# A new order table for all engines' steps in a block-sparse attention and gated feed-forward kernel

## Chip, cores and metric

The kernel runs on one core of one Trainium2 chip. The metric is the device time of one execution in microseconds (us); lower is better. A core has five engines that run their own instruction lists and meet only at semaphores: PE (TensorE, matmuls), ACT (ScalarE), DVE (VectorE), POOL (GpSimd) and SP (SyncE, which here only issues DMAs). Each engine executes its list strictly in order, so an instruction that waits holds back all that stand behind it on the same engine.

## What is computed

Two functions in a row. The first is attention with a block mask, 4 batches of 8 heads, 768 tokens, head size 64, blocks of 32 tokens:

```
scores = (q @ k.T) / 8                      # per batch and head, 768 x 768
mask   = neighbour blocks, first/last block row and column, 3 sampled blocks per row
attn   = softmax(where(mask, scores, -1e9))
x      = attn @ v                           # heads joined: (4, 768, 512)
```

The second takes x through two weight matrices with a convolution over three neighbouring tokens as a gate:

```
h    = relu(x @ w_in)                       # (4, 768, 1024)
c[t] = w[0]*h[t-1] + w[1]*h[t] + w[2]*h[t+1]  # per channel
out  = (h * sigmoid(c)) @ w_out             # (4, 768, 512), float32
```

## The kernel before

The mask costs no elementwise pass: q and k tiles have 88 rows, 64 of data and 24 that add a large negative number to masked blocks inside the score matmul itself (tiles `e` and `o`, for even and odd 128-token chunks).

The work is cut into **units** u = 0 to 143. One unit is 1024 score columns: two `s` steps on PE (L742, one for each half, 6 to 12 matmuls together) write a PSUM tile `st` (2 of them), one `exp` on ACT (L753) turns it into `pt` (6 of them), two `av` steps on PE (L775, 4 matmuls each) multiply `pt` with the values `vt` into `av`. Two heads make a pair P = 0 to 15; pair P belongs to batch P // 4. Units run by half-batches ("segments" 0 to 8, 18 units each but the last two, which have 12 and 6). When a pair's part of a segment is complete, DVE takes the reciprocal of the sums (`rcp`, L692) and scales (`norm`, L694) into `xtok`. Then `xtok` is transposed into `xT`: in segments 0, 1, 7, 8 by PE (`x_tr`, L713) with a copy (`x_cp`), in the others by a DMA transpose that SP issues (`x_xb`, L703).

From `xT` follow `f1` (PE, L864), `relu` (on ACT at L884 or DVE at L886), the gate (`mul` L916 and `add` L924 on DVE, `tanh` on ACT at L963, `g1` and `g2` on DVE; for the last segment the convolution is done by PE), `f2` (PE, L802), `ev`, a copy of the result from PSUM (ACT at L336 or DVE at L340), and `out`, the store issued by SP (L809). Out blocks of the last segments use the halves of an `st` tile as accumulators; the waits between instructions are made per tile, so the second half waits for readers of the first.

**Loads.** Pair 0 is loaded by SP and ACT at the start. All others are loads that cast to bfloat16, issued by POOL (L239): `ld_k`, `ld_q` into `nat`, `ld_nq` (second half of q) into `nq`, `ld_v` into `vn`. Pairs 1 to 5 are transposed by PE (`k_tr`, `q_tr`) and copied to `e` and `o` by `k_cp`, `q_cp` on ACT or DVE. Pairs 6 to 15 are transposed by DMA: SP issues `xb` for k and then for q (L581), DVE copies the staged tile by `stg_cp`. `v_cp` (ACT or DVE) brings `vn` into `vt`. POOL is held back by tiny copies named `pace`: the ones at L656 wait until the load three places earlier in a fixed sequence has landed, the ones at L414 wait for the `exp` of a given unit. The first of the latter is `pace` for pair 8, which waits for the `exp` of unit 40. Pair 7 is needed from the second half of unit 49 on.

**What sets the order.** The function builds a graph of 1758 named steps. Each has one or two engines to choose from, planned costs, dependencies and buffers. Nothing in the kernel schedules them: the text `ORDER` lists all steps, in the order in which they are put down, two characters for the step, one for the engine where there is a choice (P, A, V, G, S), and one for each buffer that the step takes. `put_down` reads it and emits the instructions, so each engine's list is the table's order restricted to that engine. The planned costs are not read when the program is made.

Of the kernel before, what the change touches and what calls it, by code (L numbers as in the profile page):

```python
# [25 lines left out]
6o15yV6p690Z6d6e6q05+16t04v1P05/V6i6j6u6k06y16l6v14w6z160+6m06r06s6A26nV6D00S6E0X4xhW12l06F3hZ00/6I16JhX4y2m6K4
h+hYV06R06Sh/Vi316T5i4ii06W14z176Xik6wi5Ai00iji16Y04A2x11Q1i2V6/0701RAil4B6x2116B7417111SV6C75iq1290im6G762ic1
2aV47d0idir7ein7i14C2bV2z26H7j7f36L6M1is2c04DieV6U6V6Z7k46+7n06N12eV7oit2217p5722dV7s17t24V2n023V7u0737x0iu7y2q1
2oV02B02A7z1777G16O7H784E2pV2F27g0iv7h7L07926P0io4F7l2H37M7I27a7m7q7rip07v7w7A7N37B16QV17Q12rV7R7J0W7K7b07S47V0
7C07W2kV47O2sV7X57D2C4G82183107P7E17T8407cV8707FV887Uiw7Y8918c1ix2J12I7Z8d2yV0i602GV18e28h04H7+12N08i7/i7i918j3  # L30
4Ii8V2f0ia8508m12DV1ibA8nif08o4igiy28u0iz868a8vihAiA2P8z12Q18A8w5iBiO1iG3800iP8B0iC8E02K4J2t18biH8f8FiDiI8J12S8g
8kiJ8l81A8K8piE8q18G18x8yiK2g08CiF8D2RiL8H2iViQ2hV2OA28IiMiU02EViV8L2iN2T0iW2LV2iR2X2Y18R0iSA08SiX8T38W1iYV18X
i+18Y4i/2MV8/090j0Vj109158r2941958sj22Uj71960j3V9909a8Mjm0j409b12+9h1jo2/08t29i8Njnj89j2j58O0jp9m09nj9V8U0j6A8V
319r1jq9o3ja1jbju1jd0jvjrje8P9s9w0jcAjx8Z321308+92jfA93jwjj19t49xjC2jg0jhjyiZ9y5369E1js372jkjiV9798jz9cjE9F2u0jD
9d19G09J0jA9k9KjF9l9L19e19O1jt9p9q339PjlV9u2wA9T02vAjB9U9vk819Q2jK3k9jL9z9V3jGjY0393a29Y19f9A9ZjHjMa409g9H09IjN
9M9+4jZjOa59N9R8QjI9SjP9W3c9XjJa91aaa65kajQiT9/jRj+3bab09B2ae09Cj/2VV3af9Dk0A2kb3h2WVaj1ag1k20a11a2k33d0kcA3k4
2ZA3k5jS1k6V1a30jT34V4akjUal2ar0k1jVa01asjWA0ke0kfat3jXkh1kgV1kiaw135V3kkjAax3l3kn0ay4kokC03i0kk1kEaB0kpAklkDaC
kmAa7kFa8acaG1aD5kq0kGadaHkK1kt1kH3nahkMaL0kr3o13mkLaI0aikuksVamaMkvAkNkz03eaN1aT1kOaUkw1kS2ankPkx3skIkAao0kTaY0
aV2aZkJ1au0avazaAkyVaEkBAaFaJb11kVa+3b2aKkQl61apaOb34b60kRaqb7lc0kUb85be1k+3bfl7l03pbg0aP1kWaWbj0bkaQ2aXk/kXa/b0
b4bo1aRb5b9bl1bal1aSbh0bpldkYl2bq2bt0bikZbubmbb1l3lebcby1bzbv3bdl4bnl8l5brbsbA43qV0bG0bHk7l938V43fV1bI5lf3v3w1  # L40
laV2bL1bMlgA0bwbQ03rVli1bN0lh3gVljll0kdlkV3jA0lm3AbRlblnVbV1bWbS1lr1lG0lo0lIlsbX23x3B1lplHc10c2ltV3t1lqAbxc61lJ
c33c7bBbC1lO1lx1lylKc84cb0bJlzVcclD0lLlQcg1bKlP3ychlu1cd5bD0lRbObPlvbEbTci0lElMcl0bF1lSbUcmlwAbY3KlNct13L0lTlA1
lW2bZculYcn1c40lB3zlXc5c9calFVcv33Hcy03I2czb+2lUcelZlCAmg03PlVcA4cD1cfcEl+mh3Mb/cF2cjcI0ck3uV1ma1c0m23l/cJcom3
cp1cQ1cRcK5m4cw3CcxcBm5cCcGmbcS0m0m6cV0cHcLm1cM3NcWm7c+1cq1micrcX1c/m8mccscN0m9cT0cUd03d30cOd4mjcPd54cY3Zmd3+2
mkV1d81d9meV0mm03Q0da5dg03DV2mn3JV2mo3EV423OcZmfdhd1mpdi03W3Gdl1mqV3dmmy1dn1mz3/mB0mC3X0mAA0dq0mDVd2drms1mW0ds2
mtmX3Rdv1dwmYmudx3mZmE0mv40m+431d6d7mwV2mFm/dD0dbmGVdEdI1dc1n0dF4mH1n10mIdJdd2mJAmN04cde4d3dN0dK5mOn21df2dj41dO
n3dkmK1n4dP0mL494a1n5domxdpdS1dTmPVmMA4hdtdudX0dU13SV3dYdy3TVmQ1mRdZ2n6e314e4i0e4na2dzmT0nbe53mUmSVdG0e80dHe9n7
mVVdLed1dA1eeni3ea4nw1dBdMdQdRncdVef5dCdWd+ei04fndejnq0n8ek0e00eq1neer3Fd/1n9e6e744es1ev0njewnrnkex3eA1e1eb3VeB
ecnlege2nfehel4gem3YV3et0eF0nmeC4nx4ong4p2eueyen2eznheGnneK1eonyeH5eLepnonsnpeDeEeM045V4eS0eT4jnteU2eX1nuV0eYnz
eZ14bV4eI48eJnAV2eNf00mrf1eO1eP1f5146Vf23mlf6nC0eQ47nDf74nI1eR0nEVnJfd04qV0nKAfe4kV1nL0ff5nM3Ufi1nNVnvfjnF14lV  # L50
fk0eV4nnGo60eWnBfn0fonHAo8nR0fp2nSo7fs1n+1e+e/ftnTAn/nO1fu1nPo9fx0o0fyf3nQAf4o1nU0fz3fF1oafGf8f9o2nVfH4nX1oe2fg0
fK0offLo3nYogfhfP1fa0fM5flnZVfQfmfqo4frfbobfU0o5fvfcfVnWAohoA1fR0ocfwou0om3fAodfW2g01g1onfB1fIovoig21g50oog6oBop
ojfJfNfC2fOoqfSg73fTga1fDgbfXfYokfEg30org4g8olg9gj0gkgc4osoCotowgl5fZ1go1f+gpoxgq0f/gdoDoyV3gt0gugeoM0gv24mgf0oN
ggozoOoEA1oPoFgC1oQA0gDgh1gH0giA1gIoS0gE1oToV1oUV1gJ3oWgM1oXVgNp20gO4p3pe1p51pgp6p4Apfgm1gV0p7AgngrphoY0oZpigW
o+Agso/1pu0pjp0pwoG0pvp1Ag+1g/gX5oHpm2oIpnh00oJpogwh30pph4oKA2gxpxpb1h52gF0pqoLpcp80gy2pkoRgGpdAgKgzgLgPhc1prpy
hdgQpl1gY1gZhe1h1p9psh2gR1h6ptgA1hh0paAh7gShigBAhq1h80pC3hrhj3pK0pDgT1pLh9hs4gUVhf0hz0pFhgha1hkpzhl1hbVhApEhthu
pZ1hB5hv2pGp+hwhE1pHp/VhFhN0hC1hOpAhG0q31pIpBq4pJhDpMq5Aqe1hHpNhP2hJ1hm0pQ1qfhnpRpOA3qhpSqu2ho0qgpThpA2qwhI0pW0
pUA1hKqvpXpVqihL1hQhRpYAhMVpPhS0hx1hThyAq60qjhU0q01hVVq7qR0qSq8q1qTAq9qkq2AqO0qaqPqlr31qbqX1qQVqYr4qcq+0qZAqU0qd
qVq/qm3qC1qWAqor01qDqnr50qI0r1r6r80r2rd1qpri0qqr9rer7ro1qrqxrprf1qyra0qJqsqzqtrjqEqAqBqKrbqLrcrgqFrhqMA2rqqGV0qN
rrrkqHrsA1rlrtrmA3rn  # L60
"""


# [954 lines left out]
```

## Time and profile before

| what | us |
|---|---|
| median of 3 runs | 216.7 |
| lowest, highest run | 216.12, 218.31 |
| span of the profiled execution, first to last instruction | 213.9 |
| PE busy in it (matmul) | 203.6 (95%) |
| PE weight loads busy | 154.0 (72%) |
| ACT busy | 193.5 (90%) |
| DVE busy | 186.6 (87%) |
| POOL busy | 60.4 (28%) |

The profile gives the profiled execution's own time as its span of 213.9 us; the timed runs also hold what lies around the first and last instruction, 2.8 us at the median. Busy time of PE is counted from modelled ends of pipelined matmuls. The granted TensorE clock is 1.00 over the whole span. The time from issue to landing of a DMA is given per tile as median or as least, median and most.

### The profile page before, as it was taken

The page shows a single profiled execution, that of the slowest core. Times are in us where ns is not written, and L with a number is a line of the kernel's source. Part 1 is how long each engine was busy: PE and PEld are TensorE (multiplying, and loading weights), DVE is VectorE, ACT ScalarE, POOL GpSimd, SP SyncE. Part 2 cuts the span into 40 slices and gives each one's busy share as a digit, 9 for nine tenths or more (in the row PEclk, how much of TensorE's full clock was granted, in tenths as well). Part 3 has the DMA queues.
Part 4 walks back from the last instruction along what each step waited for, and adds up shares of the span by engine and source line. Part 5 has one row for each costly group of instructions (what it writes and reads, how often), then busy time and mean ns, then how long its engine had stood idle before and what let it go on. Part 6 is the DMA issues. An engine that isn't in the chain of part 4 may idle for free.

```text
span 213.9 us, 6829 instructions
## 1 busy us (share of the span) xinstructions
PE 203.6 (95%) x2702; PEld 154.0 (72%) x2721; DVE 186.6 (87%) x577; ACT 193.5 (90%) x252; POOL 60.4 (28%) x117
## 2 busy tenths in 40 slices
...
GB/s 181 186 195 202 132 123 119 113 172 99 99 123 99 138 133 162 122 106 74 103 234 96 116 104 188 105 143 114 134 154 23 20 122 3 98 5 21 80 0 196
DMA packets 48935, 24.81 MB, mean 116 GB/s; under 512 B 35120, under 2 KB 45832, under 8 KB 48904
## 3 DMA queue, kind: packets, MB, share of 16 engines
...
q14 instruction: 10, 0.08, 0.1%
...
## 4 chain that ended last, share of the span: by engine, by line
PE 66%; DVE 24%; ACT 6%; issue 3%; ACTq 0%; DVEq 0%
PE st L742 19%; PE mix L802 16%; PE mix L864 12%; PE av L775 10%; DVE m L916 9%; ACT pt L753 4%; DVE m L924 4%; DVE hE L886 3%; PE st L802 2%; PE mix L504 2%; PE av L230 2%; DVE xtok L694 1%; DVE gT L971 1%; DVE o L340 1%; DVE e L340 1%
## 5 line engine op out<-in xcount | busy, mean ns | idle before, releaser
L753 ACT ACTIVATE pt<-st 128x1024 bf16<-128x1024 f32 x144 | 141.3, 1027 | 5.6 <-PE st L742 4.2
L775 PE MATMUL av<-vt,pt 128*128 128x65 bf16 x1152 | 60.4, 193 | 0.2
L775 PEld LDWEIGHTS <-pt 128*128 128x128 bf16 x1152 | 52.3, 97 | 10.1
L864 PE MATMUL mix<-xT,winb 128*128 128x384 bf16 (+2 forms) x288 | 52.8, 308 | 0.3 <-DVE hE L886 0.3
L916 DVE TENSOR_SCALAR m<-hE,cw 128x382 bf16<-128x382 bf16 (+2 forms) x192 | 49.4, 320 | 0.2
L802 PE MATMUL mix<-woutb,gT 128*128 128x512 bf16 x157 | 44.6, 379 | 1.6 <-DVE gT L971 0.6
L742 PE MATMUL st<-o 88*128 88x128 bf16 (+1 forms) x240 | 44.5, 229 | 0.3 <-ACT pt L753 0.2
L742 PE MATMUL st<-o,e 88*128 88x128 bf16 (+1 forms) x228 | 44.2, 233 | 0.2 <-ACT pt L753 0.2
L742 PE MATMUL st<-e,o 88*128 88x128 bf16 (+1 forms) x224 | 42.5, 234 | 1.2 <-ACT pt L753 1.1
L742 PE MATMUL st<-e 88*128 88x128 bf16 (+1 forms) x208 | 41.8, 239 | 0.4 <-ACT pt L753 0.2
L742 PEld LDWEIGHTS <-o 88*128 88x128 bf16 x464 | 34.3, 97 | 8.9 <-issue 2.0
L742 PEld LDWEIGHTS <-e 88*128 88x128 bf16 x436 | 32.9, 97 | 9.0 <-issue 0.9
L924 DVE TENSOR_TENSOR m<-m 128x764 bf16<-128x764 bf16 (+2 forms) x64 | 33.8, 533 | 0.3
L864 PEld LDWEIGHTS <-winb 128*128 128x128 bf16 x288 | 24.2, 97 | 8.2 <-issue 0.8
L963 ACT ACTIVATE m<-m 128x764 bf16<-128x764 bf16 (+2 forms) x32 | 26.3, 821 | 1.9 <-DVE m L924 1.8
L414 POOL COPY pace<-pt 1x1 bf16<-1x1 bf16 x24 | 7.6, 315 | 58.9 <-ACT pt L753 58.8
L802 PEld LDWEIGHTS <-gT 128*128 128x128 bf16 x192 | 15.7, 97 | 11.7 <-DVE gT L971 2.3
L886 DVE TENSOR_SCALAR hE<-mix 128x384 bf16<-128x384 f32 (+2 forms) x30 | 16.4, 553 | 7.9 <-PE mix L864 7.6
L884 ACT ACTIVATE hE<-mix 128x384 bf16<-128x384 f32 (+2 forms) x34 | 16.5, 492 | 3.1 <-PE mix L864 2.2
L971 DVE TENSOR_TENSOR gT<-m,hE 128x764 bf16<-128x764 bf16 (+3 forms) x36 | 18.3, 511 | 0.5
L694 DVE TENSOR_TENSOR xtok<-av,rcp 128x384 bf16<-128x384 f32 (+2 forms) x36 | 18.2, 507 | 0.4
L239 POOL DMA_DIRECT2D nat<-in_q_dram x23 | 16.9, 734 | 2.4 <-issue 1.9
...
## 6 DMA issues: line engine op xcount, KB each, us to landing
...
```

Of the source, the lines that this page charges most:

```text
L239: return op(name, {eng: occ}, lambda e: on(e).dma_start(out=dst(), in_=src), prio, deps, dma=(kind, service), **kw)
L694: nm = op("norm", {"DVE": t_dps(128 * C)}, lambda e: nc.vector.tensor_tensor(out=xtok_t[xk.index][:, 0:C].rearrange("p c h d -> p h c d"), ...
L742: nc.tensor.matmul(out=st[:, 128 * x:128 * (x + n_)], lhsT=QK[kc % 2][s][0:88, 1, hh, kc // 2, :], rhs=QK[par][s][0:88, 0, hh, idx:idx + n ...
L753: nc.scalar.activation(out=pt_t[ptb.index], in_=st_t[stb.index], func=AF.Exp, bias=0.0, scale=0.125)
L775: nc.tensor.matmul(out=o[:, off:off + 65], lhsT=pt_t[ptb.index][:, 128 * x:128 * x + 128], rhs=V_t[vslot_b[P].index][:, hh, kc, 0:65], sta ...
L802: nc.tensor.matmul(out=acc(), lhsT=gT_t[gb.index][:, ffc, 128 * t:128 * t + 128], rhs=woutb[:, ffc, :], start=(ffc == 0), stop=(ffc == NFF ...
L864: nc.tensor.matmul(out=mix_t[hb.index][:, w1 * y:w1 * y + w1], lhsT=winb[:, fc, 128 * ffc:128 * ffc + 128], rhs=xT_t[xt_buf[n].index][:, f ...
L886: nc.vector.tensor_scalar(out=dst, in0=src, scalar1=0.5, scalar2=0.0, op0=ALU.mult, op1=ALU.max)
L916: nc.vector.tensor_scalar(out=m_t[cb.index][:, x, y, 0:w], in0=hE_t[heb.index][:, f0 + y, t0 + x:t0 + x + w], scalar1=cw[:, x, f0 + y:f0 + ...
L924: nc.vector.tensor_tensor(out=m[:, a_, :, 0:w], in0=m[:, a_, :, 0:w], in1=m[:, b_, :, 0:w], op=ALU.add)
L963: th = [op("tanh", {"ACT": t_act(2 * w) + 0.04}, lambda e, cb=cb, w=w: nc.scalar.activation(out=m_t[cb.index][:, 0, :, 0:w], in_=m_t[cb.in ...
L971: nc.vector.tensor_tensor(out=gT_t[gtb.index][:, f0:f0 + 2, t0:t1], in0=m_t[cb.index][:, 0, :, 0:w], in1=hE_t[heb.index][:, f0:f0 + 2, 1 + ...
```

## The change

Only the text `ORDER` changes. All 1758 steps, their dependencies, durations, buffer counts and the code that emits them stay. The new table has the same steps in another sequence, with other choices of engine and buffer. The first lines:

```diff
 ORDER = """
-000m010g0f0n0h02030410o0i0t050p0j0q0s060zA1t00k0r070AA0l081u18A1090v1F00a0b1aA0c1H20d0N0w01bA19V1c00O0xA1i11f0
-1dV00yA0e1jV1l11eV1kA1gA0R1o00E4K11hA4L0D4P01nA1mV1B14Q4M01v10u0Q0P1I1wV14R14U11xV4V1T11y00G4W24Z01V34+1zV0F1AA
...
+000m0104105060708090a0g0n0Q0s0R0O0T0N0S0P0f0i020o0u030p0q1t01u0t0h0j0r1o01B11F01H118A20AA1aA0zA0v1bV19A2734r28
+0b0c0d1c01dV01eV0w00xA1f01i10yV1kA1jA0D1gV0E0e1l11hA1mA1nA4K14L4P04Q1v01y14M04U14R10k1sV04V0F4N04O4Z04+1wV11xV
...
```

Decoded, step by step and engine by engine, these are the differences that the prediction speaks of:

- **Engine choices.** 47 steps change engine: `relu` 10 from ACT to DVE and 8 back; `ev` 7 from DVE to ACT and 4 back; `q_cp` 4 each way; `x_cp` 3 to ACT and 2 to DVE; `v_cp` 2, `k_cp` 1, one mask copy and one cast of k to DVE, one cast of q to ACT.
- **Start.** DVE sets the constants of `vt` and `hE` (9 small memsets) ahead of the mask's own memset; PE's first k transposes stand ahead of the mask matmuls (L309); `v_cp` of pair 0 comes directly after the first mask copies instead of behind ten other DVE steps.
- **POOL.** Pair 0's and 1's second q half come before the first v load; pair 4's k and q come before pair 2's q; and the `pace` that waits for the `exp` of unit 40 stands ahead of pair 7's `ld_q` and `ld_v`, where it stood behind both. Other swaps follow between later pairs.
- **Before the first `f1` of a segment.** Between the last `av` of the four head pairs and the first `f1` PE had 10 `s`, 6 `av`, 8 `f2` and an `x_tr` in segment 6; it now has 8 `s`, 8 `av` and 4 `f2`. In segment 4 the last `norm` now stands behind one `ev` on DVE.
- **End.** All four last `ev` are on ACT (one of them was on DVE), and two `f2` of the block in `mix` are the last on PE, where the last one was an `f2` into `st`.

More of the change, by code (lines that the diff above doesn't have):

```diff
@@ L26 @@
[L26 to L60, printed above, removed]
+0m000104105060708090a0g0n0Q0s0R0O0T0N0S0P0f0i020o0u030p0q1t01u0t0h0j0r1o01B11F01H118A20AA1aA0zA0v1bV19A2734r28
@@ new lines @@
+0b0c0d1c01dV01eV0w00xA1f01i10yV1kA1jA0D1gV0E0e1l11hA1mA1nA4K14L4P04Q1v01y14M04U14R10k1sV04V0F4N04O4Z04+1wV11xV
+1AV0G1zV4W21C04/3521531p10I5b05c4S4T4X1I1T11V21W4s4Y0K5445d51qV1rV1GV11DV1EV0H5g15h1J15i05l01KV21LV5m1M05q15r
+5n1502521213144t51555615s21NV1OV2j04u155z05A5e4v0l5f0U15j5E15F1X05k5B30J1UV25700V1P14w164x2l04y2m0+585G45J05K
+1+11YV31ZV5L520V1/V5O15P0L0B05o5p5T05U4z174A2x14B2105Q05t5u4C2z14D2A0M5v126V30C5C0601615D5H5I5V10X5w1062265066
+5M5N5R5S6a16b5915x06735aV04E5yV5W6f06g5X16364686c46o16p6h55Y25Z696d6e6q06t06u6i6j5+16r06y16s6z6k06l2kV45/V6m0
@@ new lines @@
+6v16A26w6x6D06E6nV6F3hZ1hW06B6I16JhX6C0Y0W11hYV0h+0Zh/Vii0ik6K46R06G6S6H6W16X6L1Q01RV6N11SVij6T5i316/070i46Y0
+7117416M175762i00i17d07eili5Vimi2Vic1id7i17f37j6UieA6V6Z7n06+290iq17o2c17k46Oiris2aV42dV2eV2bV7s17t727377787g0
+7p52212yV023V7x02n07u024A7yin7z17h7l7G17H2q17m7q7I27927a2oV02pV7L07M7N37r7v6P02B07Q17R7S42sV7w7A7B17Jio0/2rVip0
+7V0itiu7W7C0i61i78217K7O7P6QV17D7X5ivi8V838707T7E0iw7FV7U7Y7Z7+17/88ixi917b08408917cV8c18d8e2ia8508h08i86ibViy2
+izif08m18n8j38a8018big8o48f8u08viA2C2F24F2H24GiB81ViC8g8z18kihA2P2IiG34H2N04I2Q32f18w52DV1iDiU18l8A8piV8E08q18x
@@ new lines @@
+8y8FiO08B0iHiIiJ8J1iP8K8C8D2S8G18H2J12KiEiKiL2EV8L2iF2GV1iMiN8R08SiQiW8r08W12OV2iXiR8X8T3iYA0iSV18s8Y48/0i+190
+9152LV22MVi/j10j2j0Aj3V941958I8M8N9909aj40j5960jm0jn4J2R2X9h19i2g18U08V8Z9b1jojp8O2jqj6A9j2j70j88P2hV2iAjrj9V
+ju1jv9m09n9o39r1jsja18+jd09sjbjwjx9t4jejfAjcA9w0929x9397989E19Fjj09cjk9y5jtjy2+2t02/0319d1jg1jC2jD9k9G0jzjlV9e1
+jF9J09K9l9p9L1jh9O12u09q9u9v2vA9P9Q29fjiVjA2wVjE9z9T09A9UjY19H09I9M9N9RjBjG9V39S9Y19Zk80jH9+5k9a409WjZa5a91aa
+jK3jLjMjNjO2Y13036jPa64jIjJ9X9/ab0j+39kajQjRae0kb8t22T03212U9B0kcA29g33iT8QafiZj/9Ck0V3aj1jS0akag12ZA3al2jTjU
@@ new lines @@
+k21jVk3k4jWA1k59Dk6A0ar0aske0kf3a13c372at3kh1kia01aw1axaB0a11a7a83b3h38V42VV3kgA12WVa234V435VkjVaCkk0kn1klkoay5
+aD4kpAackC0kDkEkFkG3i0kHkmVkK13d0kIkLaG1aHaL0adahaiamanau0aI0aMavkt1kq0kukMkNaN1kvAaT1aUkrao2kOaV2apksVkS2aY03k
+kw1aZk73ea30jX3l23n3m3s3t1kxkJ1kyVkTkVkUkPb11b2kz0azaAaEaFaJaq3o1kAa+3kQb353pb60b7kBAlc1k+3kWb84be1bfkRk/aKaO
+aQ0aP1aWaXa/b0b4b5b9babg0bj0bkbo1ldbpkXbl1l60l7l0l1aRbq2l2l3kYbb1kZbcl4l5bt0bubh0bibmbnby1brbz3fV0lel8bv3aSbA5
+bG0bHbI4l9lfbdk1bL1bsbMbQ0bR3jV03uV13qV13gVlgV03rVlaA1ll0lmlnVli1ljlkVlG0lHbN0bS1bV1bWbX23v3w33A3x3y3z3HbwlIc10
@@ new lines @@
+bxc2bBlo0bC1lpbD2c61c7c33lJbElqAc85lKlLlr1lsbJcb0bKbObPcccd4ltVlu0bTbUbYcg1chlO1lPlQlRlvlMci0lx1bZb+0lSlwAlycl0
+c40cmc5ct1lzVlD0culEc9lA1lBcalTlW2lYb/lXcn1cv33KlCAlUlZlNcy0czlhcecfcjckcD13B0cEcolFVcA5mg1cI0cJcp1cwm23m3l+m4
+m5lVma0cxcBcCcF23L03P3Mm6cK4l/cQ1cRcGcV0cWcHcLcMbF1lb3Cc0cS0mhmbm7m03I2cq1m1crcscX1c+1c/d03mimcm8cT0cUd30d4d55
+cN2m9mdmeV3cOd81cYmjd9mm0dg0da4mkV03Z3+1423N3/cPdhmndi0cZdl1dmdn1mod1mpkdd2d6dq0drmqA13DV23EVds33O3W3X0mB1my0mz
+dv1dw3Q1430mAA0mCd7dbmDVmW0mXmZmY40dx5dD0mH0dEdF23JV2mE1dc1mFmGAdI1djdkmImJAdJdK4dN0domN1dOmK0mLdS1dP0dp3Rm+dd0
@@ new lines @@
+n21n4m/n3dedf2mMVn0dtmOdTdudydzdG0dX0dYms04c4d24h41494e4a14f4gdU3dZ5mPAmt44mldA1n10e31e4e51n5n6n7dHe80dLe9ea2
+mQ14o4p2mRmumvdBna2ncmwA2dMdQdCnb3SV3nd3TVn8need1dRdVn9eeei0ejef4dWd+ek0mT0mUd/1e6e7ebece02mVVeq1egerev0ewehnf
+e1mSVni3njnlnkng3YV3es3nw0nq1ex1eA1eleBemet0eunheF0eyeGnmeC2eH4nrnneK1eLnxen0nyeS0ezeDeEeIeTnseM5eX1eYeU0eono
+4bV43U4i1npeZ3nznAV0nteJf00f1f5145V4e23Vmx46VepnC0eNeP14qV0eQ4j4kV0nuA24lVnvnBmreR03G3Ff21nDnEAnI1f6f72nJfd0fe
+nL0nMff4nKVnNVfi1fjeO1fk5nF1nGfn0eVfoeWe+e/fs1ftnHAo60o7o9o8nO0nPnR1fp0fu3nSfx0fyf3f4f8n+1fF1f9fg0fhflfmfqfrfv
```

12 lines of the change are left out of this document (9 added, 3 removed).

## Prediction, made before the changed kernel was run

> **What bounds the kernel now.** I read first the page's busy times and its chain of work that ended last, then the busy times by stretch, then who waited for whom, and last the timelines of POOL and of the end.
>
> ```profile
> span 213.9 us, 6829 instructions
> PE 203.6 (95%) x2702; PEld 154.0 (72%) x2721; DVE 186.6 (87%) x577; ACT 193.5 (90%) x252; POOL 60.4 (28%) x117
> ...
> PE 66%; DVE 24%; ACT 6%; issue 3%; ACTq 0%; DVEq 0%
> ```
>
> Three engines are near full, PE most. The chain runs on PE for 66% of the span. By stretch (columns: stretch, its length, busy us of PE, PEld, DVE, ACT, POOL, clock, DMA share, GB/s):
>
> ```profile
> 8.00:50.00 42.00, 40.54 (x662) 34.29 (x660) 38.54 (x124) 41.03 (x47) 22.10 (x43) 1.00 1.17 152
> 50.00:63.00 13.00, 12.84 (x160) 9.31 (x159) 11.50 (x32) 12.33 (x17) 4.21 (x8) 1.00 0.77 104
> 63.00:175.00 112.00, 109.58 (x1454) 82.68 (x1466) 101.55 (x289) 106.54 (x133) 26.84 (x50) 1.00 0.77 117
> 175.00:208.00 33.00, 32.38 (x387) 23.39 (x389) 30.26 (x111) 26.40 (x45) 0.00 (x0) 1.00 0.12 43
> ```
>
> From 8 to 50 us ACT is the bound: 41.03 of 42. The chain there alternates between PE and one `exp` after another (from 39.7 to 49.8 it is ACT alone). From 63 to 175 PE is: 109.58 of 112. In the last stretch PE (32.38 of 33) and DVE (30.26, without a gap from 176.3) are both full. The waits show how little is left:
>
> ```profile
> PE st L742 <- ACT pt L753: 1.7, 6, 0.7
> ...
> DVE hE L886 <- PE mix L864: 7.6, 8, 2.8
> ...
> ACT pt L753 <- PE st L742: 4.2, 10, 1.0
> ```
>
> DVE's largest wait is for `f1`, and costs nothing while PE is the bound. So a new order of the same steps can win a little where ACT is the bound, and loses wherever it makes PE wait.
>
> **The change part by part.** The sum is made against the span of 213.9; the median of the runs lies 2.8 above it, and I carry that over. No step is added or taken away, so only moved work and new waits have a price.
>
> *Start.* PE's first k transposes go ahead of the mask matmuls, and DVE's small memsets (0.06 to 0.08 each) ahead of the mask's memset. POOL's mask steps and so its loads start about 0.4 later, which the wait of DVE for the sampled blocks (1.13, until 3.65) covers. The first `s` needed the last of five copies behind the mask matmuls at 6.82; by the same rows it needs `q_cp` on ACT at about 6.9. If that cover were gone, the 0.4 would show. Value 0, ends -0.3 and +0.4.
>
> *ACT's stretch, 8 to 50 us.* Between the `exp` of unit 0 and that of unit 40 ACT loses two copies of q (0.27 and 0.48 from start to start in the timeline) and one `relu` (0.42): 1.17. DVE takes them, with 42.00 - 38.54 = 3.46 idle in the stretch to take them from. Ends: 0, if DVE's copies come late, and -1.2. I take -1.2 here, since ACT has hardly an idle gap and DVE has three times what it needs.
>
> *Pair 7's loads.* This is what can eat it. POOL, before:
>
> ```profile
> 41.76 0.80 POOL L239 DMA_DIRECT2D nat<-in_q_dram  x1 [0.27 <-issue]
> ...
> 44.90 0.70 POOL L239 DMA_DIRECT2D vn<-in_v_dram  x1 [0.55 <-DVE o L340]
> ...
> 51.38 0.61 POOL L414 COPY pace<-pt 1x1 bf16<-1x1 bf16 x1 [3.87 <-ACT pt L753]
> 51.92 0.72 POOL L239 DMA_DIRECT2D nat<-in_k_dram  x1
> ```
>
> The first two lines are pair 7's q and v, the third is the `pace` behind the `exp` of unit 40. It now stands ahead of both loads, and everything behind it on POOL waits with it. Pair 7's path becomes: `exp` of unit 40 ends 1.2 earlier, `pace` at 50.2, `ld_q` at 50.75. The landing times (least, median, most) of `nat`, `vn`, `stg` and `xT`, in this order:
>
> ```profile
> DMA to landing us min/median/max: 3.1/4.2/7.1
> DMA to landing us min/median/max: 4.2/5.5/7.8
> DMA to landing us min/median/max: 4.0/5.0/5.6
> DMA to landing us min/median/max: 2.3/3.9/6.0
> ```
>
> With medians q lands at 54.95, the `xb` behind it at 59.95, and two `stg_cp` (0.59 and 0.55) end at 61.1. Unit 49's second `s` started at 62.4 before, its first at 62.1. So about 1.0 of the 1.2 lives. On the way DVE, which executes in order, meets `v_cp` of pair 7: `ld_v` at about 51.9 lands at 57.4, then an `ev` (0.69) and a `norm` (0.56), at 59.0 still ahead of the staged tile; by the longest landing (7.8) it would be 61.2, about as late as the other path. What queues behind that `v_cp` is the `relu` of segment 1 and so PE's `f1`. Value -1.0 in all up to unit 49, ends -1.8 (ACT sheds 0.66 more up to unit 49: a `v_cp` of 0.72 and an `x_cp` of 0.36 against a `relu`) and +2.4 (longest landings 7.1 and 5.6: 50.75 + 12.7 + 1.1 = 64.55 against 62.1).
>
> *Transposes ahead of `f1`.* In five segments `f1` needs the last `x_xb`. Before, `f1` started 4.9, 3.1, 3.9, 4.0 and 4.0 after its issue, and PE had no gap over 0.5 there, so these bound the landing from above. In segment 6 PE now has 8 `s` x 0.22 + 8 `av` x 0.12 + 4 `f2` x 0.43 = 4.4 between the last `av` and `f1`; `rcp`, `norm` and the transpose take 0.18 + 0.56 + 3.9 = 4.6 and some 0.1 of issue: PE waits 0.3. In segment 4 the `norm` stands behind an `ev`: 0.69 + 0.56 + 3.9 = 5.2 against 4.5 of PE work: 0.7. In the others the cover is as long or longer. By a landing of 3.1 both are covered. Value +0.5, between 0 and 1.0; by the longest landing (6.0) +4.6.
>
> *63 to 175 us otherwise.* PE's steps are the same and PE had 2.4 idle; no row tells which new waits come. Value 0; ends -1.5 (most of that idle goes) and +1.5.
>
> *End.* From the first `f1` of segment 6 on PE now has 4 more `f2`, 2 more `s` and 2 fewer `av`: 1.72 + 0.44 - 0.24, about 2.0 more (an `x_tr` with it), and as much less before. With PE at 32.38 of 33 in that stretch, what comes earlier is given back. The last steps, with all `ev` on ACT:
>
> ```profile
> 209.05 0.59 ACT L336 COPY o2s<-st 128x512 f32<-128x512 f32 x1 [1.19 <-PE st L802]
> 209.69 0.59 PE L802 MATMUL st<-woutb,gT 128*128 128x512 bf16 x2 [0.72 <-ACT o2s L336]
> ...
> 210.31 0.59 ACT L336 COPY o2s<-st 128x512 f32<-128x512 f32 x1 [0.68 <-PE st L802]
> ```
>
> PE waits 0.72 here for a copy out of the other half of the same tile. That wait stays, with two `f2` into `mix` behind it: from the last `g2` 0.59 + 0.59 + 0.43 + 0.86 + 0.16 + 0.59 and some 0.1 of waits are 3.3; it was 210.9 - 207.47 = 3.43. With DVE free of its `ev`: -0.2, ends -0.8 and +0.5.
>
> Sum: 0 - 1.0 + 0.5 + 0 - 0.2 = -0.7: a span of 213.2 and a time of 216.0.
>
> **The rivals.**
>
> *Relief carried through.* ACT stays ahead past unit 49 (1.17 + 0.66, and a `relu` of 0.42 less up to unit 72: 2.25), landings are short, the end gives 0.6: 216.7 - 2.9 = 213.8. For it: ACT's 41.03 of 42, and DVE's long waits, which show slack. Against it: PE, not ACT, binds from 63 on, and pair 7's loads are late in any case.
> The Trainium skill, page "Perfetto Trace Analysis", section "Identifying the Most-Contended Engine", says that matmul busy time misjudges PE and that the weight loads' busy share is to be read. That is 72% here, below ACT's 90%, and by that rule ACT's relief would count in full and this rival hold; the trace bears it out from 8 to 50 us, while from 63 to 175 the chain runs mostly on PE.
>
> *Pair 7 late: slower.* Its place is the second half of unit 49. It decides from the point where q's landing and the staged tile's together exceed 62.1 - 50.75 - 1.1 = 10.25 us (medians 9.2, longest 12.7); at the longest it costs 2.4 and no relief is left: 219.1. For it: q, v, the next k and a half q are now issued within some 3 us, where they were spread from 41.8 to 52.9. Against it: the DMA share is only 0.77 there.
> The Trainium skill, page "DMA: Bandwidth & Descriptors", section "Issuing engines are not separate DMA queues", says that transfers from all issuers interleave on the same 16 DMA engines; by that the bunched loads and SP's transposes stretch each other, towards 219. The medians in the trace speak for 216.
>
> *`f1` waits for transposes.* Segments 4 and 6 with landings of 5 instead of 3.9 make PE wait 1.4 and 1.8, and 0.9 more in segment 5: 4.1 for 0.5, so 216.0 + 3.6 = 219.6. Against it: the last transposes of before all landed within 4.9, four of five within 4.0.
>
> That the change does nothing is excluded: 47 steps change engine and the lists of all engines differ.
>
> **How the numbers follow.** A difference under 1% (2.2 us) is about what a measurement of this kernel cannot tell from none. Chances: the forecast 0.44, from 214.6 to 217.5; relief carried through 0.29, from 211.8 to 214.5; pair 7 late 0.15 and transposes late 0.12, from 218.9 to 221. Cutting about a tenth at each side gives 212.5 to 219.5. Faster by over 1% 0.29, within 1% 0.44, slower by over 1% 0.27.
>
> **What would show it.** The `exp` of unit 40 should start near 49.0 (50.2 before). Pair 7's q load should be issued right behind the `pace` of L414, and unit 49's `s` start near 61.1; 62 or later speaks for the second rival. DVE should sit idle for some 1 us ahead of pair 7's `v_cp` or `stg_cp`. PE should show gaps of 0.3 to 0.7 before the first `f1` of segments 4 and 6. From 63 on PE's busy share should stay near 98%. I am wrong if PE's idle in the middle grows beyond 4 us, or if unit 72 comes more than 2 us earlier than its 97.0.

## The result, and the profile after

The changed kernel takes 225.0 us (median; 223.84 to 225.72) against 217.5 for the one before on the same chip: a ratio of 1.036 (1.029 to 1.043). Ratios, here and below, are of fast runs alone: this one leaves out a run of the kernel before at 221.3 us, and b_fill, with three slow runs of four, has none. The profiled execution has a span of 222.8 us against 213.9, so 8.9 us are to be explained; the forecast was a span of 213.2. (Where one execution has both a time and a span, the time lies 1.7 to 2.1 above the span, so some 0.8 of the 2.8 that the forecast carried over was a difference between executions.)

The page of the profile after, its head and the chain that ended last by engine:

```profile
span 222.8 us, 6862 instructions
...
PE 210.1 (94%) x2721; PEld 156.6 (70%) x2721; DVE 188.1 (84%) x579; ACT 192.3 (86%) x250; POOL 60.9 (27%) x117
...
PE 45%; DVE 27%; ACT 12%; DMA 10%; issue 4%; SPq 0%; ACTq 0%; DVEq 0%
```

The busy times of ACT and DVE have hardly moved. PE's is 6.5 us longer; part of that is matmuls at a lower clock, as shown below. What has moved is the chain. PE's share of it fell from 66% to 45%, and DVE (27%) and DMA (10%, none before) took its place. The busy times by stretch show the same as idle PE (the stretches of before, and the same columns):

```profile
8.00:50.00 42.00, 41.35 (x644) 35.19 (x645) 37.96 (x113) 38.16 (x45) 19.07 (x39) 1.00 1.11 144
50.00:63.00 13.00, 12.81 (x166) 9.37 (x163) 11.99 (x35) 12.40 (x16) 6.21 (x11) 1.00 0.59 66
63.00:175.00 112.00, 107.64 (x1399) 79.70 (x1397) 97.49 (x280) 101.83 (x129) 29.06 (x52) 0.98 0.85 119
```

From 63 to 175 PE is idle 4.36 of 112 (2.42 before; the forecast had named 4 as a sign of being wrong) and issues 69 weight loads fewer. The clock column reads 0.98: one stretch in it ran slower. The waits name the new one:

```profile
DVE hE L886 <- PE mix L864: 6.1, 6, 4.0
...
DVE e L340 <- DMA stg<-nat: 2.9, 2, 2.6
...
PE st L742 <- DVE e L340: 1.8, 2, 1.4
```

DVE waits 2.6 us once for a staged tile (`stg`), and PE waits 1.4 for DVE's copy of it. DVE's old wait for `f1` fell from 7.6 to 6.1: part of its slack was spent.

Where the 8.9 arises is read from the start of each unit's `exp`, changed kernel against before: +2.2 at unit 8, +3.1 at unit 40, +7.0 at unit 60, +5.9 at unit 100, +7.8 at unit 143, +8.9 at the end.

One thing has to be known to read these numbers. The moment from which PE's clock is granted in full differs between executions of one and the same first steps: in the profiled ones it was 5.7, 12.8 and 20.4 us for three kernels that all begin in the order of before, and then unit 8 came 0, 1.9 and 4.9 later. So a kernel's loss is counted from unit 8 to the end below, and the start by itself.

### The profile page after: what moved, and what is told of

It is laid out like the page before. It is cut to its first block, busy times and chain, and to the rows that moved or that the text cites. A ratio compares the mean times of both kernels' runs of the same rounds, so it can differ in the third digit from the quotient of the medians.

```text
span 222.8 us, 6862 instructions
## 1 busy us (share of the span) xinstructions
PE 210.1 (94%) x2721; PEld 156.6 (70%) x2721; DVE 188.1 (84%) x579; ACT 192.3 (86%) x250; POOL 60.9 (27%) x117
## 4 chain that ended last, share of the span: by engine, by line
PE 45%; DVE 27%; ACT 12%; DMA 10%; issue 4%; SPq 0%; ACTq 0%; DVEq 0%
PE st L742 14%; PE mix L802 11%; DVE m L916 8%; PE mix L864 8%; PE av L775 6%; ACT pt L753 6%; DMA stg<-nat 5%; DVE m L924 4%; DMA xT<-xtok 4%; DVE hE L886 3%; DVE e L340 2%; ACT m L963 2%; DVE o L340 2%; DVE gT L971 2%; PE st L802 2%
## 5 line engine op out<-in xcount | busy, mean ns | idle before, releaser
L775 PE MATMUL av<-vt,pt 128*128 128x65 bf16 x1152 | 59.0, 194 | 0.1
L775 PEld LDWEIGHTS <-pt 128*128 128x128 bf16 x1152 | 51.3, 98 | 8.7 <-ACT pt L753 0.7
L864 PE MATMUL mix<-xT,winb 128*128 128x384 bf16 (+2 forms) x288 | 54.7, 310 | 1.3 <-DMA xT<-xtok 0.9
L916 DVE TENSOR_SCALAR m<-hE,cw 128x382 bf16<-128x382 bf16 (+2 forms) x192 | 50.2, 320 | 1.0 <-ACT hE L884 0.6
L802 PE MATMUL mix<-woutb,gT 128*128 128x512 bf16 x176 | 47.3, 380 | 1.7 <-DVE gT L971 1.1
L742 PE MATMUL st<-o,e 88*128 88x128 bf16 (+1 forms) x228 | 45.1, 236 | 0.8 <-DVE o L340 0.5
L742 PE MATMUL st<-e 88*128 88x128 bf16 (+1 forms) x208 | 43.2, 245 | 1.9 <-DVE e L340 1.8
L742 PEld LDWEIGHTS <-e 88*128 88x128 bf16 x436 | 33.5, 99 | 12.7 <-DVE e L340 2.3
L414 POOL COPY pace<-pt 1x1 bf16<-1x1 bf16 x24 | 8.3, 344 | 65.4 <-ACT pt L753 65.2
L886 DVE TENSOR_SCALAR hE<-mix 128x384 bf16<-128x384 f32 (+1 forms) x32 | 17.5, 550 | 7.3 <-PE mix L864 6.1
```

Of the source, the lines that this page charges most:

```text
L742: nc.tensor.matmul(out=st[:, 128 * x:128 * (x + n_)], lhsT=QK[kc % 2][s][0:88, 1, hh, kc // 2, :], rhs=QK[par][s][0:88, 0, hh, idx:idx + n ...
L775: nc.tensor.matmul(out=o[:, off:off + 65], lhsT=pt_t[ptb.index][:, 128 * x:128 * x + 128], rhs=V_t[vslot_b[P].index][:, hh, kc, 0:65], sta ...
L802: nc.tensor.matmul(out=acc(), lhsT=gT_t[gb.index][:, ffc, 128 * t:128 * t + 128], rhs=woutb[:, ffc, :], start=(ffc == 0), stop=(ffc == NFF ...
L864: nc.tensor.matmul(out=mix_t[hb.index][:, w1 * y:w1 * y + w1], lhsT=winb[:, fc, 128 * ffc:128 * ffc + 128], rhs=xT_t[xt_buf[n].index][:, f ...
L886: nc.vector.tensor_scalar(out=dst, in0=src, scalar1=0.5, scalar2=0.0, op0=ALU.mult, op1=ALU.max)
L916: nc.vector.tensor_scalar(out=m_t[cb.index][:, x, y, 0:w], in0=hE_t[heb.index][:, f0 + y, t0 + x:t0 + x + w], scalar1=cw[:, x, f0 + y:f0 + ...
```

## The experiments

All times are of the profiled executions, in us, as differences to the kernel before. The ratio is that of the timed runs to those of the kernel before on the same chip.

| kernel | unit 8 | unit 40 | unit 60 | unit 143 | end | from unit 8 to the end | ratio |
|---|---|---|---|---|---|---|---|
| changed | +2.2 | +3.1 | +7.0 | +7.8 | +8.9 | +6.7 | 1.036 (1.029 to 1.043) |
| a_start | +0.3 | +0.7 | +3.4 | +5.2 | +6.3 | +6.0 | 1.021 (1.007 to 1.035) |
| a_warm | +1.2 | +2.3 | +5.8 | +7.0 | +8.0 | +6.8 | 1.034 (1.025 to 1.042) |
| a_act | +1.9 | +2.5 | +6.2 | +7.8 | +8.8 | +6.9 | 1.030 (1.022 to 1.038) |
| a_pace | +2.3 | +2.8 | +2.8 | +4.6 | +5.7 | +3.4 | 1.017 (1.004 to 1.031) |
| a_both | +0.1 | +0.5 | +0.5 | +1.7 | +2.8 | +2.7 | 1.010 (1.002 to 1.019) |
| a_q | +0.3 | +0.7 | +0.9 | +1.8 | +2.8 | +2.5 | 1.012 (1.007 to 1.018) |
| b_pace | +0.5 | +0.5 | +5.7 | +5.7 | +5.8 | +5.3 | 1.018 (1.010 to 1.026) |
| b_fill | +4.8 | +4.8 | +8.1 | +8.1 | +8.1 | +3.3 | - |
| c_norm | +3.8 | +3.7 | +3.7 | +5.9 | +7.0 | +3.2 | 1.023 (1.014 to 1.033) |
| f_relu | +1.9 | +2.7 | +2.7 | +4.3 | +5.3 | +3.4 | 1.015 (1.007 to 1.023) |
| f_relu_tail | +2.0 | +2.8 | +2.8 | +4.5 | +4.8 | +2.8 | 1.012 (1.002 to 1.022) |
| e_order | +0.8 | +3.9 | +3.3 | +19.0 | +21.2 | +20.4 | 1.106 (1.096 to 1.115) |
| e_eng | +3.9 | +4.6 | +6.5 | +10.5 | +10.8 | +6.9 | 1.048 (1.044 to 1.053) |
| d_front | +1.8 | +2.4 | +2.4 | +5.0 | +4.2 | +2.4 | 1.012 (1.007 to 1.017) |
| d_back | +1.9 | +1.9 | +1.9 | +4.0 | +5.0 | +3.1 | 1.011 (1.002 to 1.019) |
| d_end | +0.3 | +0.5 | +0.5 | +1.8 | +2.8 | +2.5 | 1.012 (1.006 to 1.018) |
| b_tail | +4.9 | +4.9 | +4.9 | +4.9 | +4.1 | -0.8 | 1.001 (0.995 to 1.006) |

The theory before the experiments: the start costs up to 2.9, pair 7's late q load costs some 4, and the order of the middle the rest. The rival: the loss is spread over the whole order, and mending any one place moves the wait elsewhere. Most edits below are moves of steps in the table (the number in brackets is the head pair, or the unit that a `pace` waits for); a_warm and b_fill add matmuls, b_tail and f_relu_tail change a buffer. Kernels with the same order but another start differ too: a_pace and a_both stand at +3.4 and +2.7 in the last column but one, so a difference of less than 0.7 between kernels with different starts says little.

### Pair 7's loads: a_pace, a_q, b_pace, b_fill

```diff
 POOL, changed kernel (a_pace)
-pace(unit 40), ld_q(7), pace, ld_v(7), pace, ld_k, ld_nq
+ld_q(7), pace, ld_v(7), pace(unit 40), pace, ld_k, ld_nq
 POOL, a_both with the pace in between (a_q)
+ld_q(7), pace(unit 40), pace, ld_v(7), pace, ld_k, ld_nq
```

> The changed kernel with one POOL instruction moved: the pace copy that waits for the exp of unit 40 stands again behind pair 7's loads of q and v. Theory: DVE's wait of 2.64 us for pair 7's staged tile, PE's gaps of 1.6 and 0.7 at 64.5 and 66.2 and the half clock that follows from 67.9 to 71.3 all go; unit 52, which is 5.9 us behind the kernel before, is then 2.2 behind, and the span falls by 3.5 to 4 to about 219. Rival: DVE and ACT are so full there that another wait takes its place (f1, or pair 8's tile); then the span falls by 1.5 or less.

Measured: a span of 219.6, a little less of a fall (3.2) than the theory's 3.5 to 4, and unit 60 at +2.8 instead of +7.0. The move of one `pace` is worth 3.3 from unit 8 to the end (6.7 - 3.4; with a_start's edits as well, 6.0 - 2.7, again 3.3). The place in the changed kernel, first POOL and then DVE:

```profile
54.46 0.46 POOL L414 COPY pace<-pt 1x1 bf16<-1x1 bf16 x1 [11.20 <-ACT pt L753]
54.92 1.19 POOL L239 DMA_DIRECT2D nat<-in_q_dram  x1
56.10 0.18 POOL L656 COPY pace<-vn 1x1 bf16<-1x1 bf16 x1
56.22 0.70 POOL L239 DMA_DIRECT2D vn<-in_v_dram  x1
```

```profile
60.64 0.33 DVE L340 COPY vt<-vn 128x768 bf16<-128x768 bf16 x1
61.75 0.69 DVE L340 COPY o2s<-mix 128x512 f32<-128x512 f32 x1 [0.78 <-PE mix L802]
62.36 0.55 DVE L694 TENSOR_TENSOR xtok<-av,rcp 128x384 bf16<-128x384 f32 x1
65.55 0.55 DVE L340 COPY e<-stg 64x1536 bf16<-64x1536 bf16 x1 [2.64 <-DMA stg<-nat]
66.13 0.77 DVE L340 COPY o<-stg 64x1536 bf16<-64x1536 bf16 x1
66.83 0.54 DVE L886 TENSOR_SCALAR hE<-mix 128x384 bf16<-128x384 f32 x1
```

POOL stood 11.20 us at the `pace` with pair 7's loads behind it. q was issued at 54.92 and its transpose at 59.16 (4.24 later, the median of before); the chain of waits then holds one piece of DMA, and PE's second `s` of unit 49 starts at 66.16:

```profile
59.16 6.30 DMA stg<-nat
```

6.30 is longer than the longest landing of `stg` before (5.6). The Trainium skill, page "DMA: Bandwidth & Descriptors", section "Issuing engines are not separate DMA queues", has all issuers' transfers interleave on the same engines; this row, with five loads issued from 54.92 to 60, fits, but no run here shows which transfer stretched it. In the four kernels of the changed order that keep the `pace` ahead of q this transpose took 5.86 to 6.30, and 2.75 and 4.40 in a_pace and a_both. The load of q ahead of it went the other way: 4.1 to 4.3 in the four, 5.5 and 6.2 in the two. Together the two landings took 10.1 to 10.5 in the four, 8.4 in a_pace and 10.8 in a_both, so the bunch does not make the sum long.

> a_both (216.7 span) with the pace of unit 40 behind pair 7's q load but still ahead of its v load: q and so the staged tile are early, v is issued some 7 us later (about 52.5 instead of 45.3). Theory: q, its transposes and the staged tile are what made unit 49 late, v lands by 58 where its copy on DVE starts at 57.7 in a_both: unit 49 within 0.5 of a_both's -0.7, span 216.7 to 217.2. Rival: the copy of v, which DVE meets first, holds DVE up as well (by its longest landing of 7.8 until 60.3): unit 49 at +1 to +2, span 218.5 to 219.5.

Measured: a_q ends where a_both does (216.7), though v is issued some 7 us later. So q with its transpose is the whole of it; the copy of v that DVE meets first was not late.

> The kernel before with one part of the change: the pace copy for unit 40 stands ahead of pair 7's loads of q and v on POOL, all else as before. Theory: q is issued at about 52 instead of 41.8, its transposed tile lands near 62 to 63, the copies of it end past 63 where unit 49 needs them at 62.1, and the value copy on ACT waits 2 us; the span grows by 2 to 4, more if PE's clock drops in the gap. Rival: the loss of the changed kernel needs its denser order of DVE as well; then the span grows by less than 1.

```diff
 POOL, kernel before (b_pace)
-ld_q(7), pace, ld_v(7), pace, ld_nq(4), pace(unit 40)
+pace(unit 40), ld_q(7), pace, ld_v(7), pace, ld_nq(4)
```

Measured: +5.7 from unit 48 on, constant to the end: in this kernel nothing behind unit 48 takes a delay up. It came from another load than expected: the half q of pair 4 (`nq`), third in the queue behind the `pace`, which was moved with the rest:

```profile
59.44 0.85 PE L504 MATMUL mix<-ident,nq 128*64 128x128 bf16 x6 [3.90 <-DMA nq<-in_q_dram]
```

The wait is 3.90 and the loss 5.3 from unit 8: more than the wait. b_fill asks whether the difference is PE's clock.

```diff
 q_tr of pair 4, second half (b_fill)
+for _ in range(16):
+    nc.tensor.matmul(out=mix[:, 0:512], lhsT=warm[:, 0:128], rhs=warm, ...)
```

> The kernel before with the five POOL steps behind the pace (as in b_pace, 219.7 span, +5.7 from unit 48 to the end), and with 16 matmuls of 512 columns that compute nothing needed, put on PE into the 4.07 us in which it waited for the half q of pair 4. The wait itself stays: the load is not earlier. Theory: 1.7 of the 5.7 is the granted clock of 0.5 for the 3.4 us behind the wait; with PE kept busy there is no slot of 0.5 at 59 us, +4.0 from unit 48 on, and the span is about 218.0. Rival: all 5.7 is the wait and the work behind it: 219.7 again, or more by what the filler delays.

The stretch from 59 to 63 us of b_pace, then of b_fill (same columns as above):

```profile
59.00:63.00 4.00, 3.56 (x27) 2.21 (x28) 2.46 (x6) 0.16 (x1) 0.87 (x2) 0.57 1.54 155
```

```profile
59.00:63.00 4.00, 3.95 (x38) 2.08 (x35) 1.35 (x4) 3.04 (x6) 2.53 (x6) 1.00 1.37 177
```

With the wait filled by useless matmuls the clock stays at 1.00 and the loss from unit 8 is 3.3 instead of 5.3. Not all of these 2.0 are clock. The load was meant to be no earlier, but it landed 4.1 us after its issue, in b_pace 5.2. So in b_fill nothing waits for it any more; the transposes follow the filler at once:

```profile
59.16 0.65 PE L778 MATMUL av<-vt,pt 128*128 128x65 bf16 x16
59.64 3.62 PE L501 MATMUL mix<-warm 128*128 128x512 bf16 x15
63.19 0.52 PE L507 MATMUL mix<-ident,nq 128*64 128x128 bf16 x6
```

From the start of the last `av` to the transposes it is 4.03 here and 4.55 in b_pace (54.89 to 59.44). That is 0.5 of the 2.0; 1.4 to 1.5 is left for the slower clock, of the 1.7 expected (3.4 us at half clock lose at most that). The changed kernel has the lower clock too, behind its waits of 1.44 and 0.52 at unit 49:

```profile
68.00:71.00 3.00, 3.00 (x28) 2.12 (x27) 2.73 (x9) 2.11 (x4) 0.18 (x1) 0.50 0.65 79
```

In a_start the same place has waits of 0.97 and 0.30 and no lower clock, and units 40 to 60 cost 2.7 instead of 3.9: of the 1.2 between them 0.7 is the shorter waits, and the rest is put down to the clock, which no run here separates.

### The start: a_start, a_both, a_warm, a_act

```diff
 ACT
-cast_q, m_k, cast_k, m_k
+m_k, m_k, cast_q, cast_k          (a_act; a_start, a_both too)
 PE
-k_tr, w24 (mask matmuls)
+w24, k_tr                         (a_start and a_both only)
```

> The changed kernel with its start alone set right: on ACT the two mask copies stand again ahead of the first cast of q, which waits 0.90 us for its load, and on PE the mask matmuls (L309) stand again ahead of the first k transposes. Theory: the start costs the changed kernel about 2.5 us, 1.7 by this order (first exp at 9.6 instead of 7.9) and the rest because PE sits idle for 0.96 us after the warm-up matmuls and is granted full clock only from 13.2 us (5.7 before). Then the first exp is back near 8.0, full clock comes by about 6, and the span falls from 222.8 to about 220.3. Rival: the loss is only handed on, since pair 7's loads wait for the exp of unit 40 and f1 for transposes; then the exps up to unit 40 come 2 us earlier and the span falls by under 1.

Measured: span 220.2 and unit 8 at +0.3: the number was met, and yet the reason was not what it seemed. The full clock came at 6.1 instead of 13.2.

> Both repairs together. Theory: they add up, 6 to 6.5 us: a span of about 216.5, still some 2.5 above the 213.9 of the kernel before, by waits that are spread over the rest (f1 behind transposes, units 104 to 116, the end). Rival: they do not add up, because the earlier start makes pair 7 earlier by itself; then the span is 218 to 219.

Measured: 216.7, +0.1 at unit 8 (full clock from 4.3).

> The changed kernel with four more 256-column warm-up matmuls on PE ahead of the first k transposes, where PE idles 0.96 us; nothing else. Theory: of the 2.9 us that unit 4's exp is late, 1.7 (unit 0's lateness) is the order of the first steps, and 1.2 is PE's clock, which was granted in full only from 13.2 us on, since the idle 0.96 us broke the run of matmuls. Then the granted clock is full from 5 to 6.5 us on, unit 0 stays +1.7, unit 4 falls to about +1.7, and the span to about 221.6. Rival: the clock is a by-product and the order alone makes all of the 2.9: unit 4 stays at +2.9 and the span at 222.8.

The four matmuls stand on PE behind the first transposes, so the idle time ahead of these was not filled (its row shows 0.56, that of the changed kernel 0.65). All the same the clock was full early, at 5.5, unit 4 came at +1.8, and the span was 221.9. So that idle time alone does not make the clock late. Nor is the change needed for it: d_back, which begins in the order of before, has the same late clock. Whether the changed first steps make it more likely stays open: they had it late both times that they were profiled as they are (13.2 and 13.3). The stretch from 6 to 13 us of before, of the changed kernel, of a_warm and of d_back:

```profile
6.00:13.00 7.00, 5.89 (x70) 4.33 (x69) 6.47 (x19) 6.84 (x13) 5.76 (x9) 1.00 1.37 186
```

```profile
6.00:13.00 7.00, 7.00 (x56) 5.30 (x56) 5.91 (x13) 4.67 (x11) 5.79 (x9) 1.00 1.32 174
```

```profile
6.00:13.00 7.00, 5.87 (x72) 4.44 (x70) 6.29 (x13) 5.76 (x12) 6.45 (x11) 1.00 1.32 171
```

```profile
6.00:13.00 7.00, 7.00 (x51) 5.20 (x49) 5.06 (x17) 5.48 (x11) 5.10 (x8) 1.00 1.35 194
```

PE does 70 and 72 matmuls in 5.9 us in two of them, 56 and 51 in 7.0 in the other two. The clock column reads 1.00 in all four, because the trace has no clock entry before the first full grant (so the kernel before did not have the full clock over its whole span either, but from 5.7 us on); the matmuls tell it (128 columns start 107 ns apart in the changed kernel until 13 us, 56 ns from there on).

> The changed kernel with only ACT's two mask copies put back ahead of the first cast of q; PE's first k transposes stay ahead of the mask matmuls (a_start moved both). Theory: what costs is ACT's 0.90 us of waiting for q with the copies behind it; the k transposes then start at about 5.5 as in a_start, the mask matmuls behind them at 5.8, and of the 1.2 us that a_start won by unit 8 at least 0.8 come back: unit 0 at +1.2, unit 8 at about +0.6 where the granted clock is full from 6 us on. Rival: PE's order is the cost, since the mask matmuls had their operand at 4.8 and now wait for the k transposes: nothing comes back, unit 8 +1.2 as in a_warm.

Measured: full clock from 12.9, unit 0 at +1.3, unit 8 at +1.9. The latter is what d_back shows at the same clock without any change of the start; so between ACT's and PE's order nothing is told apart. What the order of the first steps costs at unit 8 is read at like clocks. With a late one the changed steps stand at +2.2 against d_back's +1.9: 0.3, and the 1.9 is the clock. With an early one they stand at +1.2 (a_warm, which has its four matmuls on top) against +0.1 to +0.3 mended: up to 1.0.

### The middle and the end: c_norm, f_relu, e_order, e_eng, d_front, d_back, d_end, b_tail, f_relu_tail

a_both still loses 2.7. The first suspects were PE's waits for `f1` behind the last transposes of a segment.

```diff
 DVE, a_both (c_norm)
-rcp, g2, norm          (segment 3)
+rcp, norm, g2
-rcp, g2, ev, norm      (segment 4)
+rcp, norm, g2, ev
 DVE, a_both (f_relu)
-stg_cp, stg_cp, relu, relu     (segment 5)
+relu, stg_cp, stg_cp, relu
```

> a_both (216.7 span) with two norm steps on DVE put directly behind their rcp: in segment 3 ahead of one g2, in segment 4 ahead of one g2 and one ev. Theory: the waits of PE for f1 there (0.56 and 0.44) come from DVE's order, since the last transpose leaves 0.5 and 1.4 earlier now: both go, unit 116 falls from +1.5 to about +0.5, and the span to about 215.8. Rival: PE's wait only moves to the f2 that need the g2, or to the buffer that the ev frees: span 216.4 to 216.9.

Measured: +3.2 from unit 8, no gain. PE's waits for the transposes of segments 3 and 4 (in a_both 0.39 at 105.89 and 0.27 at 130.03) are gone, and there is a new one for `g2`, at an `f2` ahead of the first place:

```profile
105.39 1.04 PE L802 MATMUL mix<-woutb,gT 128*128 128x512 bf16 x4 [0.56 <-DVE gT L971]
```

> a_both with two stg_cp on DVE put behind one relu of segment 5: DVE stood idle 0.92 for their staged tile with that relu behind them, and PE 0.79 for the f1 that needs its buffer. Theory: of the 2.7 that a_both loses from unit 8 to the end, this wait is 0.8 to 1.0: unit 124 falls from +1.9 against unit 8 to +1.0, the end from +2.7 to about +1.8. Rival: the lost time is DVE's work itself, and the wait moves to the next step that DVE brings late (f2 behind g2, as in c_norm): the end stays within 0.3 of +2.7.

The wait in a_both, DVE's side and then PE's:

```profile
155.76 0.55 DVE L340 COPY e<-stg 64x1536 bf16<-64x1536 bf16 x1 [0.92 <-DMA stg<-nat]
156.33 0.56 DVE L340 COPY o<-stg 64x1536 bf16<-64x1536 bf16 x1
156.80 1.01 DVE L886 TENSOR_SCALAR hE<-mix 128x384 bf16<-128x384 f32 x2
```

```profile
157.41 0.81 PE L864 MATMUL mix<-xT,winb 128*128 128x384 bf16 x4 [0.79 <-DVE hE L886]
```

In f_relu the relu is no longer behind the copies, and PE waits at the same place all the same, for the transposes now; +3.4 from unit 8:

```profile
157.13 0.65 PE L864 MATMUL mix<-xT,winb 128*128 128x384 bf16 x3 [1.06 <-DMA xT<-xtok]
```

Twice a wait was taken away and the time stayed (f_relu and a_pace, which begin alike with a late clock, both stand at +3.4): the rival holds in the middle.

```diff
 e_order: a_both's order, every step on the engine of before
 e_eng:   the order of before, 48 steps on the engines of the changed kernel
```

> a_both's order (+2.7 from unit 8 to the end of the span) with every step on the engine that it has in the kernel before: 48 steps go back (on ACT again: most copies of q, four relu; on DVE again: six ev). Theory: DVE took ACT's place on the path from 30.8 to 40.4 us in a_both, and with the copies back on ACT unit 40 is no later than in before; what is lost behind unit 100 is order, and stays: +2 to +3 from unit 8 to the end. Rival: the engines are the loss: within 1 of before from unit 8 to the end.

> The kernel before, its order kept, with the 48 steps on the engines that the changed kernel gives them. Theory: the engines alone move little: within 1 us of before from unit 8 to the end, and unit 40 no earlier than before, since PE, not ACT, sets the pace (PE idles only 1.46 of the 42 us). Rival, the prediction's step: ACT's relief brings unit 40 forward by about 1.2 against unit 8.

The two tables differ in 48 engine choices; the 47 named ahead of the prediction is one short of its own list. Both kernels fell far outside: +20.4 and +6.9 from unit 8, where the two changes together lose 2.7. So order and engines depend on each other, and their shares can't be separated so. One thing e_eng does say: with the order of before and ACT relieved (its busy time from unit 8 to 40 falls from 33.17 to 32.61), these units take 34.5 us, against 33.9 before. ACT's relief buys nothing in that order either.

```diff
 d_front: a_both up to the exp of unit 100, then the order of before; last sums in two tiles
 d_back:  before up to the exp of unit 100, then a_both's order
 d_end:   before up to the exp of unit 128, then a_both's order
```

> a_both's order up to the exp of unit 100, where it stands 0.8 ahead of the kernel before, then the order of before for all steps that are left, and the last but one output block in another pair of banks (as in b_tail, -0.8). Theory: the loss of a_both behind unit 100 (+3.6) lies in its own order of those steps: the lead of 0.8 lives, span 213.9 - 0.8 - 0.8 = 212.3. Rival: the lead is borrowed, by DVE and PE work that a_both put behind unit 100: it is paid back within some 20 units, and the span is 213.1 or more.

> The kernel before up to the exp of unit 100, then a_both's order for all steps that are left. Theory: the loss is in the order behind unit 100: +2.5 at the last exp and +3.6 at the end, span 217.5. Rival: the debt was made ahead of unit 100; from before's state a_both's order does no harm: span 214 to 215.

> The kernel before up to the exp of unit 128, then a_both's order for all that is left. Theory: the end of a_both loses 0.8 by its own order of the last steps (unit 128 +2.0, the end +2.8): 0.8 from unit 8 to the end here too. Rival: the end of a_both only carries out what was left over before: within 0.3 of before.

d_front: the lead of 0.8 is not kept; it stands at +1.3 at unit 100 (with a start of +1.8) and at +5.0 at unit 143, 3.7 lost under the order of before. So the lead was borrowed. The steps started by then say from whom: at the `exp` of unit 100 a_both has done 44 `f2` and the kernel before 48, which are 1.7 us of PE (4 x 0.43). That is more than the lead, but not all of the 3.7: PE waits 1.08 at 145.69, behind the cut, which neither whole order does. d_back loses 3.1 and so lies near its theory (+3.6), and d_end 2.5, which would put all of a_both's loss behind unit 128. But the shares do not add up: in d_end ACT waits 1.63 for an `av` at the seam, a wait that neither whole order has, so the cut itself costs. d_end is inconclusive.

```diff
 f2 of the last but one output block (b_tail, f_relu_tail; in d_front too)
-tail buffer 1, in f_relu_tail 0 (a half of tile st0, which holds the other sum too)
+tail buffer 2 (first half of tile st1)
```

> The kernel before with the last but one output block's sum in another pair of banks (buffer 2 instead of 1 of the tail, so the two last sums do not share a tile); order unchanged. Theory: PE's wait of 0.72 ahead of the last two f2 (for the copy out of the other half of the same tile) goes, ACT's two last copies become the path: span 213.9 - 0.5 to 213.9 - 0.7, 213.3. Rival: ACT's copies and the last store were the end anyway, and the span stays 213.9.

> f_relu with the last but one output block in another pair of banks (as in b_tail). Theory: the two add: another 0.8 off the end, +1.0 from unit 8 to the end, a span of 215.0 where the start is as in a_both. Rival: the end is set by f2 waiting for g2 there (0.91 in a_both), so the banks matter little: less than 0.4 off.

Measured: PE's wait of 0.72 is gone in both; b_tail ends 0.8 earlier than before counted from unit 8, f_relu_tail 0.6 earlier than f_relu. The changed kernel kept that wait, as forecast:

```profile
217.65 0.59 PE L802 MATMUL st<-woutb,gT 128*128 128x512 bf16 x2 [0.72 <-ACT o2s L336]
```

Counted from unit 8, b_tail is the best version by its trace, but its ratio to before is 1.001 (0.995 to 1.006): 0.8 us is less than these runs resolve.

## Why the prediction was wrong, step by step

Of the 8.9 us, 2.2 stand at unit 8 (1.9 of them a late clock that the order of before can have too), 3.3 are the `pace` put ahead of pair 7's loads, and 3.4 the rest of the new order. The forecast was -0.7.

**Pair 7's loads (forecast -1.0 at unit 49, measured +4.4 there and +7.0 at unit 60): the step that failed.** The path was laid out rightly, `pace`, q, its transpose, two copies, second half of unit 49, and so was the median landing of q (4.2). Three terms were wrong. It began at an `exp` of unit 40 that was to be 1.2 earlier than before and came 3.1 later (start and ACT's stretch, below). The staged tile took 6.30 instead of its median of 5.0, past the longest seen. And a price was missing: PE's clock at 0.50 behind its wait. q's landing and the tile's together were 10.54, past the 10.25 from which the second rival was to decide; it is this rival that happened, at the place named. From unit 40 to unit 49 the changed kernel loses 1.3 where a_pace gains 1.2: a price of 2.5, where this rival had 2.4. To the end the `pace` costs 3.3. Its chance of 0.15 was too little: 10.25 lies only 1.05 above the sum of two medians, and the two landings together took 8.4 to 10.8 in these runs, bunched or not.

**ACT's stretch (forecast -1.2): nothing came.** From unit 8 to unit 40 ACT's busy time fell from 33.17 to 32.58 us (of the three steps taken off it only the `relu` lies there; the two copies of q lie ahead of unit 8, where the clock covers what they gave; the rows from 8 to 50 us show a larger fall because the changed kernel is late in them), and these units took 0.9 longer (a_both: 0.5). The bound was misread: before, PE was busy 33.56 of the 33.91 us from unit 8 to unit 40, so no relief elsewhere could have given more than 0.35 there. What the change did was to put DVE on the path, from 33.1 to 43.4 us. A part of the chain, where before it ran on PE and then on one `exp` after another:

```profile
36.78 0.56 DVE m L924
37.34 0.47 DVE hE L886
37.81 0.46 DVE m L924
38.27 0.48 DVE hE L886
38.75 0.03 issue
38.78 0.79 DVE m L916 x2
39.57 0.46 DVE xtok L694
40.03 0.93 DVE m L916 x4
```

The 3.46 us that DVE had idle were counted as if it could use them anywhere; its steps stand in a queue, and each copy that it took pushed the `mul` and `add` behind it. The prediction's own row already gave a warning: PE was busy 40.54 of the same 42, so the forecast needed 1.2 of PE's 1.46 of idle time to be waits for ACT.

**Start (forecast 0, ends -0.3 and +0.4):** 0.3 with a late clock, inside the ends; up to 1.0 with an early one (a_warm), outside them. The +2.2 at unit 8 is mostly the late clock, which the prediction did not know and which comes with the order of before as well.

**Transposes ahead of `f1` (forecast +0.5):** PE's gap in segment 4 appeared; that in segment 6 did not, and one came in segment 3 instead. In all PE waits 0.9 for `xT`. But c_norm shows that this wait is not a price of its own: taken away, another stands in its place.

**63 to 175 otherwise (0, ends -1.5 and +1.5) and the end (-0.2):** from unit 60 to 143 a_both loses 1.2, inside the ends, and from there 1.1 where -0.2 was forecast. By the `exp` of unit 143 it has started 150 matmuls of `f2`, before 153: some 0.65 of the 1.1 is PE work put off, as the forecast said of this stretch (what comes earlier is given back). Beside it PE has a wait of 0.74 for `g2` at 196.45 that before does not have and the forecast did not name. The wait for the copy of the last output block (b_tail) was named rightly.

What stays open: which order of which steps makes the 2.7 of a_both. Two single waits were shown not to be it, and the cuts and the exchange of engines make waits of their own. An estimate can say where it arises: if the matmuls that a_both has started more or fewer by then are counted at their mean spacing in the trace (`f2` 0.22, `f1` 0.14, `s` 0.07, `av` 0.03), its loss from unit 8 is some 0.5 at unit 100, 1.1 at unit 116, 2.0 at unit 124 and 2.4 at unit 143. So about half of the 2.7 arises between units 100 and 124.
